# Two tiles of x on ScalarE's load queue, more softmax buffers and another order of the instructions in a fused attention and dense kernel

## The chip, the cores and the metric

The kernel runs on one core of a Trainium2 chip. The metric is device time in microseconds (us). A core has five engines that each work through a queue of their own in order: TensorE (matmuls; PE in the profile, its weight loads PEld), VectorE (DVE), ScalarE (ACT), GpSimd (POOL) and SyncE (SP, which here only issues DMAs). Sixteen DMA engines move the data. SP and ScalarE can both issue loads, each on a queue of its own.

## The reference

The input x has 2048 tokens of 512 features (bf16). After a layer norm without scale, two branches are added to x:

```python
xn = layernorm(x)
# A: linear attention, 32 heads of 16 features
q, k, v = split(xn @ wqkv)
phi(t)  = concat(softmax(t @ w_phi), softmax(-(t @ w_phi)))     # per head, 16 + 16
kv  = sum over tokens of phi(k)^T v;   z = sum over tokens of phi(k)
o   = (phi(q) @ kv) / (phi(q) . z + 1e-6)
A   = o @ wo
# B: dense layer with mish
h   = xn @ w1 + b1              # 1792 features
B   = (h * tanh(softplus(h))) @ w2
out = x + A + B
```

## The kernel before

The tokens stand in 16 tiles of 128. Four tiles form a group g. TensorE needs xn with features on the partitions (`xnT`); for group 0 it is turned by TensorE itself (TP, L557) and copied out of PSUM (TC, L564), for the other groups by DMA (`ln_turn_dma`, L185, part of AP).

The matrix w_phi is folded into the weights of q and k: `load_turned` (L140) loads 512 columns of wqkv transposed by a DMA into `wT`, F0 and F (L152) multiply it with `Wbd`, a block diagonal matrix that WB (L523) makes of w_phi, and FD and FC (L164) copy the products into `wkp` and `wqk`. Logits of tile i and softmax group s (0 to 3 keys, 4 to 7 queries) then are one product (L, L246; LP for the first two tiles at once, L202; WL for two tiles of group 1), copied by LC.

Each softmax group goes through E (maximum and minimum, and differences from them), X (exponentials, ScalarE), S (sums, L302, VectorE), R (inverses, L325) or W (weights for the queries, L347), N (products). A collects kv on TensorE; KV masks it. Of the queries, W ends with two DMA transposes (L290), Q multiplies with kv, G copies the results, C divides and turns them by DMA (L440). H is one block of 128 of the 1792 hidden features for one group (56 in all), M its mish on ScalarE. O is the second dense layer of a tile, P adds the attention's projection, Y adds x and stores. The last tile is done in two parts (OH, PH, YH). V and VC are the values, LN and AP statistics and normalisation of groups 1 to 3; for group 0, LS, RS and AZ do the same tile by tile. PB and CB turn the bias b1, DX loads groups 2 and 3 of x, DW 2 and DW 3 load w2 and wo, WT loads the q columns of wqkv transposed, KM makes a mask.

The order of all this is a list written out (`STEPS`, L24): every step emits its instructions to its engines at that place, so each engine's queue has the order of the list. A number behind @ is the PSUM bank (six in rotation, each of 512 columns); a or v says whether ScalarE or VectorE does a copy or an inverse. A step waits only for its data and for its bank or buffer to come free. Ahead of the list stand the first loads and twelve matmuls on constants (L511):

```python
    nc.sync.dma_start(x_sb[:, 0, :], x_v[:, 0, :])
    wT_of = {0: load_turned(D)}
    ...
        nc.scalar.dma_start(wsrc[:], wphi_v)
    nc.scalar.dma_start(x_sb[:, 1, :], x_v[:, 1, :])
    nc.scalar.dma_start(b1b[:], b1_v[:, :])
    nc.sync.dma_start(x_sb[:, 2:4, :], x_v[:, 2:4, :])
    nc.sync.dma_start(wv[:], wqkv_v[:, :, 2 * D : 3 * D])
    nc.sync.dma_start(w1_sb[:, :, 0 : 7 * P], w1_v[:, :, 0 : 7 * P])
    nc.sync.dma_start(x_sb[:, 4:8, :], x_v[:, 4:8, :])
    nc.sync.dma_start(w1_sb[:, :, 7 * P : F], w1_v[:, :, 7 * P : F])
```

The old list begins: LS 0; RS 0; DX 2; LS 1; WB; RS 1; AZ 0; TP 0; F0 0; F0 1; AZ 1; FD 0 v; TP 1; TC 1 v; LS 2; PB; RS 2; TC 0 a; LS 3; RS 3; FD 1 a; AZ 2; F0 2; F0 3; FD 2 a; FD 3 a; LP; KM; DX 3; AZ 3; V 0; LC 0 0 a; TP 2; V 1; TC 2 a; TP 3; VC 0 a; LC 0 1 v; TC 3 v; CB; L 0 2; L 0 3; LC 0 3 a; LN 1; H 0; H 1; H 2; M 0.

Of the kernel before, what the change touches and what calls it, by code (L numbers as in the profile page):

```python
# [8 lines left out]
BF16 = mybir.dt.bfloat16  # L9
# [12 lines left out]

WARM = 12
STEPS = """  # L24
LS 0; RS 0; DX 2; LS 1; WB; RS 1; AZ 0; TP 0 @0; F0 0 @1; F0 1 @2; AZ 1; FD 0 v; TP 1 @3; TC 1 v; LS
2; PB @4; RS 2; TC 0 a; LS 3; RS 3; FD 1 a; AZ 2; F0 2 @5; F0 3 @0; FD 2 a; FD 3 a; LP i @1,2; KM;
DX 3; AZ 3; V 0 @3; LC 0 0 a; TP 2 @5; V 1 @0; TC 2 a; TP 3 @1; VC 0 a; LC 0 1 v; TC 3 v; CB; L 0 2
@5; L 0 3 @2; LC 0 3 a; LN 1; H 0 @3; H 1 @1; H 2 @4; M 0; LC 0 2 a; H 3 @2; M 1; M 2; M 3; VC 1 a;
E 0 0; H 4 @3; H 5 @5; AP 1 0; H 6 @1; H 7 @4; M 4; H 8 @2; M 5; H 9 @0; M 6; M 7; H 10 @3; M 8; M
9; M 10; AP 1 1; H 11 @5; E 0 1; V 4 @1; X 0 1; WL 1; LN 2; V 6 @4; VC 4 a; X 0 0; L 1 0 @2; L 1 3  # L30
@0; LC 1 0 a; V 5 @3; LN 3; VC 5 a; H 12 @1; WL 2; H 13 @2; VC 6 a; S 0 0; LC 1 3 a; M 11; V 3 @3; M
12; M 13; H 14 @4; H 15 @0; H 16 @5; H 17 @1; VC 3 a; M 14; H 18 @2; M 15; M 16; M 17; LC 1 2 a; H
19 @3; AP 2 0; AP 2 1; AP 3 0; L 2 0 @4; LC 2 0 a; L 2 1 @0; LC 2 1 a; V 2 @5; S 0 1; L 2 2 @1; M
18; LC 1 1 a; M 19; H 20 @4; LC 2 2 a; AP 3 1; H 21 @0; WT; H 22 @2; M 20; VC 2 a; R 0 1 v; L 2 3
@3; H 23 @1; R 0 0 v; N 0 1; M 21; N 0 0; H 24 @4; M 22; LC 2 3 a; F 0 @5; F 1 @0; E 1 0; E 1 1; M
23; M 24; F 2 @2; E 2 0; E 2 1; FC 0 a; H 25 @3; H 26 @1; FC 1 a; H 27 @4; M 25; M 26; L 3 2 @5; FC
2 a; M 27; V 7 @0; L 3 3 @3; V 11 @1; F 3 @2; L 3 0 @4; LC 3 0 v; LC 3 2 a; L 3 1 @5; A 0 0; X 1 0;
X 1 1; A 0 1; LC 3 3 a; FC 3 v; S 1 0; V 8 @4; LC 3 1 a; VC 7 a; L 4 0 @2; E 3 0; VC 8 a; LC 4 0 a;
L 4 1 @3; LC 4 1 a; L 4 3 @5; VC 11 a; L 4 2 @0; X 2 0; V 9 @4; L 5 0 @2; H 28 @3; H 29 @1; VC 9 a;
LC 4 2 v; M 28; M 29; H 30 @0; H 31 @4; H 32 @3; M 30; H 33 @1; H 34 @0; M 31; M 32; M 33; M 34; H  # L40
35 @4; M 35; H 36 @3; M 36; S 1 1; LC 4 3 a; R 1 0 v; E 3 1; LC 5 0 a; N 1 0; R 1 1 v; H 37 @1; H 38
@0; H 39 @4; H 40 @3; H 41 @5; H 42 @2; S 2 0; A 1 0; M 37; N 1 1; M 38; M 39; M 40; A 1 1; M 41; M
42; X 3 0; L 6 3 @1; L 5 2 @0; V 10 @4; VC 10 a; L 5 1 @3; LC 5 2 a; L 6 0 @5; E 4 0; E 4 1; X 2 1;
S 3 0; V 15 @2; VC 15 a; V 13 @4; VC 13 a; LC 6 0 a; R 2 0 a; S 2 1; DW 3; R 3 0 a; X 3 1; L 6 1 @0;
LC 5 1 a; DW 2; N 3 0; N 2 0; L 5 3 @2; O 0 @4; S 3 1; V 12 @5; V 14 @3; LC 6 1 a; LC 5 3 a; O 1 @0;
L 6 2 @2; R 2 1 a; N 2 1; VC 14 a; LC 6 3 a; VC 12 v; R 3 1 a; N 3 1; X 4 0; A 2 0; S 4 0; LC 6 2 a;
A 2 1; A 3 0; W 4 0 v; X 4 1; H 43 @3; M 43; A 3 1; H 44 @1; H 45 @5; M 44; H 46 @2; M 45; H 47 @3;
M 46; M 47; H 48 @1; KV; H 49 @5; H 50 @2; Q 0 0; M 48; M 49; G 0 0; M 50; H 51 @3; H 52 @1; H 53
@5; S 4 1; W 4 1 v; M 51; M 52; H 54 @2; H 55 @3; Q 0 1; M 53; E 5 0; E 5 1; M 54; E 6 0; L 7 0 @1;
M 55; G 0 1; C 0 a; X 5 0; LC 7 0 a; L 7 1 @5; X 5 1; O 2 @2; O 3 @3; LC 7 1 a; L 7 2 @1; LC 7 2 a;  # L50
S 5 0; Q 1 0; L 7 3 @5; G 1 0; E 6 1; W 5 0 a; P 0; P 1; Y 0; Q 1 1; O 4 @1; G 1 1; LC 7 3 a; O 5
@4; S 5 1; Q 2 0; O 6 @5; C 1 a; P 2; G 2 0; W 5 1 v; Y 1; Q 2 1; P 3; O 7 @0; E 7 0; X 6 0; S 6 0;
G 2 1; Q 3 0; C 2 a; G 3 0; Y 2; Y 3; X 6 1; O 8 @2; Q 3 1; W 6 0 v; E 7 1; S 6 1; P 4; P 5; G 3 1;
C 3 a; Q 4 0; X 7 0; Y 4; W 6 1 v; X 7 1; S 7 0; O 9 @3; O 10 @1; G 4 0; Q 4 1; P 6; P 7; G 4 1; Y
5; Y 6; C 4 a; Q 5 0; W 7 0 a; G 5 0; O 11 @4; Q 5 1; Y 7; O 12 @5; S 7 1; G 5 1; C 5 a; Q 6 0; G 6
0; O 13 @0; Q 6 1; G 6 1; W 7 1 v; P 8; P 9; Q 7 0; C 6 a; G 7 0; P 10; P 11; Y 8; Q 7 1; G 7 1; O
14 @2; Y 9; Y 10; C 7 a; P 12; P 13; OH 0 @3; PH 0; Y 11; P 14; OH 1 @1; PH 1; Y 12; Y 13; YH 0; Y
14; YH 1
"""


# [1 line left out]
def kernel(  # L63
# [12 lines left out]
    nc = tc.nc  # L76
# [146 lines left out]
    def hidden(u, b):  # L223
# [3 lines left out]
        for kt in range(KT):  # L227
# [5 lines left out]
                stop=(kt == KT - 1),  # L233
            )

    def mish(u):
        g, f = divmod(u, FT)
        table("mish")
        nc.scalar.activation(  # L239
            acts[:, f, g * 512 : (g + 1) * 512], ph_of.pop(u)[:], ACT.Mish, bias=b1f[:, f : f + 1]  # L240
        )
# [59 lines left out]

    def sums(s, k):  # L302

        t = s_of[s, k] = smx.tile([P, 128], FP32, name="s", bufs=3)
        nc.vector.reduce_sum(  # L305
            t[:], pair(s, k).rearrange("p t j l (c e) -> p (t j l c) e", e=16), axis=AX.X
        )
# [7 lines left out]
            out, src.rearrange("p (c o) -> p c o", o=1).to_broadcast([P, n, 2]), ACT.Exp, scale=scale  # L315
        )

    def log(src, n):

        table("natural_log_exp_and_others")  # L320
        t = smx.tile([P, 128], FP32, name="log")
        nc.scalar.activation(t[:, 0:n], src, ACT.Ln)
        return t[:, 0:n]

    def invert(s, k, how):  # L325

        t = s_of.pop((s, k))
        r2 = r_of[s, k] = smx.tile([P, 128, 2], BF16, name="r2")
        if how == "a":
            power(r2[:], log(t[:], 128), 128, -1.0)  # L330
            return
        r = smx.tile([P, 128], BF16, name="r")
        with nc.allow_low_precision("the softmaxes are bf16"):
            nc.vector.reciprocal(r[:], t[:])
        nc.vector.tensor_copy(r2[:], r[:].rearrange("p (c o) -> p c o", o=1).to_broadcast([P, 128, 2]))
# [9 lines left out]
    def weigh(s, k, how):  # L345

        t = s_of.pop((s, k))  # L347
        q = smx.tile([P, 16, 4], FP32, name="q")
        r2 = smx.tile([P, 16, 4, 2], BF16, name="q2")
        if how == "a":  # L350
            t4 = log(t[:], 128).rearrange("p (t l c) -> p t l c", l=2, c=4)
            nc.vector.tensor_tensor(
                out=q[:], in0=t4[:, :, 0, :], in1=t4[:, :, 1, :], op=ALU.subtract
            )
            power(r2[:].rearrange("p t c o -> p (t c) o"), q[:].rearrange("p t c -> p (t c)"), 64, 1.0)
        else:
            t4 = t[:].rearrange("p (t l c) -> p t l c", l=2, c=4)
            nc.vector.reciprocal(q[:], t4[:, :, 1, :])
            nc.vector.tensor_tensor(
                out=r2[:], in0=t4[:, :, 0, :, None].to_broadcast([P, 16, 4, 2]),  # L360
                in1=q[:, :, :, None].to_broadcast([P, 16, 4, 2]), op=ALU.mult,
            )
        vv = pair(s, k).rearrange("p t j l c -> p (t j) l c")[:, :, 1, :].rearrange(
            "p t (c e o) -> p t c e o", e=8, o=2
        )
        nc.vector.tensor_tensor(
            out=vv, in0=vv, in1=r2[:, :, :, None, :].to_broadcast([P, 16, 4, 8, 2]), op=ALU.mult
        )
        turn(s, k)
# [70 lines left out]
    def combine(h, how):  # L440

        nm, ds = nd_of.pop(h)
        oT_of[h] = xnT[:, 2 * h : 2 * h + 2, :, :].rearrange("p t k c -> p (t k) c")
        f = opool.tile([P, 64, 2], BF16, name="f")
        d = ds[:].rearrange("p i j c -> p (i j c)")
        if how == "a":
            power(f[:], log(d, 64), 64, -1.0)
        else:
            w = opool.tile([P, 64], FP32, name="w")
            nc.vector.reciprocal(w[:], d)  # L450
            nc.vector.tensor_copy(
                f[:], w[:].rearrange("p (c o) -> p c o", o=1).to_broadcast([P, 64, 2])
            )
        v = nm.rearrange("p i j (c e o) -> p (i j c) e o", e=8, o=2)
        nc.vector.tensor_tensor(
            out=v, in0=v, in1=f[:, :, None, :].to_broadcast([P, 64, 8, 2]), op=ALU.mult
        )
        nc.sync.dma_start_transpose(out=oT_of[h], in_=nm.rearrange("p i j c -> p (i j c)"))
# [26 lines left out]
    with nc.allow_non_contiguous_dma(reason="tiny w_phi load"):  # L485
        nc.scalar.dma_start(wsrc[:], wphi_v)
    nc.scalar.dma_start(x_sb[:, 1, :], x_v[:, 1, :])
    nc.scalar.dma_start(b1b[:], b1_v[:, :])
    nc.sync.dma_start(x_sb[:, 2:4, :], x_v[:, 2:4, :])
    nc.sync.dma_start(wv[:], wqkv_v[:, :, 2 * D : 3 * D])  # L490
    nc.sync.dma_start(w1_sb[:, :, 0 : 7 * P], w1_v[:, :, 0 : 7 * P])
    nc.sync.dma_start(x_sb[:, 4:8, :], x_v[:, 4:8, :])
# [71 lines left out]
    def first_keep(i, copy):  # L564
        copy(xnT[:, i, :, :], pf_of.pop(("t", i))[:].rearrange("p (k c) -> p k c", k=KT))

    def stats(g):
        ln_of[g] = moments_of()
        st, mv, rstd = ln_of[g]
# [30 lines left out]
    def load_queries():  # L600
# [8 lines left out]
        "LN": stats, "AP": apply, "DX": load_tokens, "DW": load_weights, "WL": wide,  # L609
        "L": logits, "LC": lambda s, i, c: take(s, i, copies[c]),  # L610
        "V": value, "VC": lambda t, c: keep(t, copies[c]),
        "H": hidden, "M": mish,
        "E": extremes, "X": exponentials, "S": sums,
        "R": invert, "N": normalise, "A": accumulate,
        "KV": mask_kv, "W": weigh, "Q": attend, "G": gather, "C": combine,
# [40 lines left out]
```

## Time and profile before

| | |
|---|---|
| Runs | 173.78, 173.88, 173.98 us, median 173.88 |
| Profiled execution | 174.0 us |
| Its span (first to last instruction) | 172.3 us |
| TensorE clock granted (mean) | 1.00 |
| Busy: PE, DVE, ACT, POOL | 168.7, 143.2, 119.5, 9.4 us |
| Read from HBM, written | 6.84 MB, 2.10 MB |

The page gives busy times of the engines, the chain of work that ended last, the costliest groups of instructions and the DMA issues. The trace behind it answers for stretches of time, single lines, waits and loads. In lists of instructions the first column is the start in us from the beginning of the span, the second the length; in brackets stands the idle time before and what ended it. "DMA to landing" is from the issue to the moment that the data can be used.

### The profile page before, as it was taken

How to read it: one execution, taken by the hardware profiler on the slowest of the kernel's cores; microseconds unless marked ns; L12 is line 12 of the kernel's file. 1: busy time of each engine (PE TensorE's matmuls, PEld its weight loads, DVE VectorE, ACT ScalarE, POOL GpSimd, SP SyncE). 2: the span in 40 equal slices, each digit the busy share in tenths (PEclk: the TensorE clock that was granted, in tenths of full speed). 3: DMA queues.
4: the chain of work that ended last, by engine and by line, in shares of the span. 5: the costliest groups of instructions: out<-in, count | busy, mean ns of one | idle time of the engine just before them, and what ended most of it. 6: DMA issues, size and time to landing. Idle time of an engine off the chain costs nothing.

```text
span 172.3 us, 2713 instructions
## 1 busy us (share of the span) xinstructions
PE 168.7 (98%) x1039; PEld 82.4 (48%) x1039; DVE 143.2 (83%) x221; ACT 119.5 (69%) x192; POOL 9.4 (5%) x26
## 2 busy tenths in 40 slices
PE   8999999999999999999999999999999999999993
PEld 2554444444545444454446544444444545445452
DVE  2878998999997999979999999799988996844433
ACT  2446889979899998989999988974063883414200
POOL 4332205000000000000000000000000000000000
PEclk9999999999999999999999999999999999999999
DMA  5999350199930000000000363023974749885641
GB/s 98 269 377 365 82 98 0 37 189 207 366 120 0 0 4 0 0 0 0 4 0 0 64 118 66 12 51 67 150 152 93 150 95 144 172 168 100 173 134 61
DMA packets 44953, 18.02 MB, mean 105 GB/s; under 512 B 37004, under 2 KB 44940, under 8 KB 44940
## 3 DMA queue, kind: packets, MB, share of 16 engines
q1 hardware_dynamic: 44096, 17.60, 44.5%
q10 hardware_dynamic: 844, 0.25, 0.6%
q8 instruction: 8, 0.13, 0.3%
q14 instruction: 5, 0.04, 0.1%
HBM read 6.84 MB, written 2.10 MB: 52 GB/s over the span
## 4 chain that ended last, share of the span: by engine, by line
PE 95%; DMA 3%; SPq 0%; DVE 0%; issue 0%
PE po L463 28%; PE ph L228 28%; PE pl L194 14%; PE po L470 8%; PE pv L194 8%; DMA wT<-in_A_wqkv_dram 3%; PE pnd L418 2%; PE pkv L387 2%; PE pfold L156 1%; PE pwide L194 1%; PE pl L209 1%; PE ptr L560 0%; SPq L483 0%; DVE x_sb L477 0%; PE pb L533 0%
## 5 line engine op out<-in xcount | busy, mean ns | idle before, releaser
L463 PE MATMUL po<-w_sb,acts 128*128 128x512 bf16 (+2 forms) x238 | 50.7, 366 | 0.0
L228 PE MATMUL ph<-xnT,w_sb 128*128 128x512 bf16 x224 | 50.1, 379 | 0.0
L239 ACT ACTIVATE acts<-ph,b1f 128x512 bf16<-128x512 f32 x56 | 37.2, 694 | 4.6 <-PE ph L228 4.4
L305 DVE TENSOR_REDUCE s<-e 128x128 f32<-128x2048 bf16 x16 | 36.4, 2279 | 2.5 <-ACT e L288 2.5
L228 PEld LDWEIGHTS <-w_sb 128*128 128x128 bf16 x224 | 21.7, 98 | 25.5
L463 PEld LDWEIGHTS <-acts 128*128 128x128 bf16 x238 | 22.3, 98 | 24.1
L288 ACT ACTIVATE e<-e 128x2048 bf16<-128x2048 bf16 x16 | 30.3, 1908 | 0.0
L194 PEld LDWEIGHTS <-xnT 128*128 128x128 bf16 x184 | 17.6, 98 | 20.1 <-DMA wv<-in_A_wqkv_dram 0.2
L252 ACT CAST p_sb<-pl 128x512 bf16<-128x512 f32 x27 | 15.4, 587 | 5.5 <-PE pl L194 4.7
L433 ACT COPY ds<-pnd 128x32 f32<-128x32 f32 x16 | 2.9, 183 | 23.5 <-PE pnd L418 23.5
L194 PE MATMUL pv<-wv,xnT 128*128 128x512 bf16 x64 | 16.1, 379 | 0.0
L477 DVE TENSOR_TENSOR x_sb<-po,x_sb 128x512 bf16<-128x512 f32 (+2 forms) x17 | 10.9, 654 | 5.7 <-PE po L470 5.7
L470 PE MATMUL po<-wqk,xnT 128*128 128x512 bf16 (+2 forms) x68 | 15.5, 366 | 0.0
L194 PE MATMUL pl<-wqk,xnT 128*128 128x512 bf16 x64 | 15.3, 379 | 0.0
L170 DVE BATCH_NORM_STATS2 stats<-x_sb 128x6 f32<-128x512 bf16 x16 | 10.1, 679 | 4.3 <-DMA x_sb<-in_A_x_dram 4.3
L263 DVE TENSOR_TENSOR m<-m 128x512 bf16<-128x512 bf16 (+1 forms) x32 | 11.5, 358 | 1.1
L194 PE MATMUL pl<-wkp,xnT 128*128 128x512 bf16 x48 | 11.7, 379 | 0.0
L263 DVE TENSOR_TENSOR m<-p_sb 128x1024 bf16<-128x1024 bf16 x16 | 10.9, 682 | 0.2 <-ACT p_sb L252 0.2
L272 DVE TENSOR_TENSOR e<-p_sb,m 128x2048 bf16<-128x2048 bf16 x8 | 9.8, 1226 | 1.4 <-PE pkv L387 1.1
L272 DVE TENSOR_TENSOR e<-m,p_sb 128x2048 bf16<-128x2048 bf16 x8 | 9.8, 1225 | 0.3
L340 DVE TENSOR_TENSOR e<-e,r 128x2048 bf16<-128x2048 bf16 x8 | 9.6, 1215 | 0.0
L138 ACT ACT_TABLE_LOAD x7 | 9.0, 1283 | 0.1
(62 smaller groups left out, 131.4 us busy)
## 6 DMA issues: line engine op xcount, KB each, us to landing
out_dram<-x_sb SPq DMA_DIRECT2D x15, 128.0 KB, 2.0
w_sb<-in_B_w_dram SPq DMA_DIRECT2D x2, 896.0 KB, 7.8
x_sb<-in_A_x_dram SPq DMA_DIRECT2D x3, 512.0 KB, 10.0
w_sb<-in_B_w_dram SPq DMA_DIRECT2D x2, 640.0 KB, 8.8
wv<-in_A_wqkv_dram SPq DMA_DIRECT2D x1, 512.0 KB, 4.5
wqk<-in_A_wo_dram SPq DMA_DIRECT2D x1, 512.0 KB, 4.6
w_sb<-in_B_w_dram SPq DMA_DIRECT2D x1, 512.0 KB, 9.6
x_sb<-in_A_x_dram SPq DMA_DIRECT2D x1, 256.0 KB, 3.2
```

The costliest lines, as they stand in the source:

```text
L170: nc.vector.bn_stats(stats[:, i, :], xs[:, i, :])
L194: nc.tensor.matmul(pp, lhsT=xnT[:, t, kt, :], rhs=w[:, kt, :], start=(kt == 0), stop=(kt == KT - 1),)
L228: nc.tensor.matmul(ph_of[u][:], lhsT=w1_sb[:, kt, f * P : (f + 1) * P], rhs=xnT[:, g * TPG : (g + 1) * TPG, kt, :], start=(kt == 0), stop= ...
L239: nc.scalar.activation(acts[:, f, g * 512 : (g + 1) * 512], ph_of.pop(u)[:], ACT.Mish, bias=b1f[:, f : f + 1])
L252: copy(p_of[s][:, i, :], pl_of.pop((s, i)))
L263: nc.vector.tensor_tensor(out=m[:], in0=src[:, :, 0:half], in1=src[:, :, half : 2 * half], op=op)
L272: nc.vector.tensor_tensor(out=e_of[s][:].rearrange("p t j l c -> p (t j) l c")[:, :, pl, :].rearrange("p t (c e o) -> p t c e o", e=8, o=2 ...
L288: nc.scalar.activation(v, v, ACT.Exp)
L305: nc.vector.reduce_sum(t[:], pair(s, k).rearrange("p t j l (c e) -> p (t j l c) e", e=16), axis=AX.X)
L463: nc.tensor.matmul(po_of[t, c.stop][:, c], lhsT=acts[:, f, t * P : (t + 1) * P], rhs=w2_sb[:, f, c], start=(f == 0), stop=False,)
L470: nc.tensor.matmul(po_of[t, c.stop][:, c], lhsT=oT_of[t // 2][:, t % 2 * 4 + j, :], rhs=wo_sb[:, j, c], start=False, stop=(j == 3),)
L477: nc.vector.tensor_tensor(out=y, in0=po_of.pop((t, c.stop))[:, c], in1=y, op=ALU.add)
```

## The change

Tiles 2 and 3 of x are loaded from ScalarE's queue, behind tile 1, and the bias behind them; they had been on SP's queue between wT and wv. The sums `s` get six buffers instead of three, `r2` three instead of two, `r` one instead of two; `log` works in place instead of into a tile of its own. Two functions are new (`hidden_half`, `first_turn_dma`) and used by no step. The list has the same 433 steps in another order, with other banks and, for some, the other engine: R 1 0, R 1 1, W 6 0 and FC 3 go to ScalarE; C 0, W 5 0 and W 7 0 to VectorE; of the copies TC 2, VC 2, VC 4 and VC 5, FD 2, LC 3 1 and LC 4 3 are now VectorE's, and VC 12, FD 0, LC 0 1 and LC 3 0 are ScalarE's.

```diff
 STEPS = """
+DX 2; LS 0; WB; DX 3; LS 1; RS 0; RS 1; AZ 0; TP 0 @0; LS 2; AZ 1; TP 1 @1; F0 0 @2; F0 1 @3; F0 2
+@4; LS 3; RS 2; AZ 2; RS 3; TC 1 v; TC 0 a; FD 0 a; FD 2 v; F0 3 @5; AZ 3; TP 2 @0; FD 1 a; FD 3 a;
+TC 2 v; LP i @2,1; TP 3 @3; TC 3 v; V 0 @4; PB @5; H 0 @0; LC 0 0 a; CB; LC 0 1 a; V 3 @2; VC 3 a; M
+0; L 0 2 @3; LN 1; LC 0 2 a; L 0 3 @1; LC 0 3 a; V 1 @5; H 1 @2; H 2 @0; DW 3; H 3 @3; H 4 @1; M 1;
+M 2; M 3; M 4; VC 0 a; H 5 @2; LN 2; H 6 @0; M 5; AP 1 0; H 7 @3; H 8 @1; AP 1 1; M 6; M 7; VC 1 a;
+H 9 @4; H 10 @2; H 11 @0; M 8; E 0 0; M 9; M 10; M 11; E 0 1; AP 2 0; H 12 @3; H 13 @5; L 1 0 @1; V
...
+0; Q 6 1; P 8; W 7 1 v; Y 8; G 6 1; P 9; P 10; Q 7 0; C 6 a; P 11; G 7 0; Y 9; Q 7 1; O 14 @3; P 12;
+P 13; Y 10; Y 11; OH 0 @2; G 7 1; C 7 a; P 14; PH 0; OH 1 @0; PH 1; Y 12; Y 13; Y 14; YH 0; YH 1
 """
...
-        t = s_of[s, k] = smx.tile([P, 128], FP32, name="s", bufs=3)
+        t = s_of[s, k] = smx.tile([P, 128], FP32, name="s", bufs=6)
...
-    def log(src, n):
+    def log(v):
 
         table("natural_log_exp_and_others")
-        t = smx.tile([P, 128], FP32, name="log")
-        nc.scalar.activation(t[:, 0:n], src, ACT.Ln)
-        return t[:, 0:n]
+        nc.scalar.activation(v, v, ACT.Ln)
+        return v
...
-        r2 = r_of[s, k] = smx.tile([P, 128, 2], BF16, name="r2")
+        r2 = r_of[s, k] = smx.tile([P, 128, 2], BF16, name="r2", bufs=3)
         if how == "a":
-            power(r2[:], log(t[:], 128), 128, -1.0)
+            power(r2[:], log(t[:]), 128, -1.0)
             return
-        r = smx.tile([P, 128], BF16, name="r")
+        r = smx.tile([P, 128], BF16, name="r", bufs=1)
...
     nc.scalar.dma_start(x_sb[:, 1, :], x_v[:, 1, :])
+    nc.scalar.dma_start(x_sb[:, 2:4, :], x_v[:, 2:4, :])
     nc.scalar.dma_start(b1b[:], b1_v[:, :])
-    nc.sync.dma_start(x_sb[:, 2:4, :], x_v[:, 2:4, :])
     nc.sync.dma_start(wv[:], wqkv_v[:, :, 2 * D : 3 * D])
```

In the old list wo's load (DW 3) comes behind S 2 1 and the load of w2 (DW 2) behind LC 5 1; in the new one DW 3 stands behind H 2 and DW 2 behind M 15. The transposed load WT comes right behind AP 3 1 instead of one H later.

The end of the old list, for comparison: Q 6 1; G 6 1; W 7 1 v; P 8; P 9; Q 7 0; C 6 a; G 7 0; P 10; P 11; Y 8; Q 7 1; G 7 1; O 14; Y 9; Y 10; C 7 a; P 12; P 13; OH 0; PH 0; Y 11; P 14; OH 1; PH 1; Y 12; Y 13; YH 0; Y 14; YH 1.

More of the change, by code (lines that the diff above doesn't have):

```diff
@@ L24 @@
 STEPS = """
[L25 to L58, printed above, removed]
+DX 2; LS 0; WB; DX 3; LS 1; RS 0; RS 1; AZ 0; TP 0 @0; LS 2; AZ 1; TP 1 @1; F0 0 @2; F0 1 @3; F0 2
+@4; LS 3; RS 2; AZ 2; RS 3; TC 1 v; TC 0 a; FD 0 a; FD 2 v; F0 3 @5; AZ 3; TP 2 @0; FD 1 a; FD 3 a;
@@ new lines @@
+TC 2 v; LP i @2,1; TP 3 @3; TC 3 v; V 0 @4; PB @5; H 0 @0; LC 0 0 a; CB; LC 0 1 a; V 3 @2; VC 3 a; M
+0; L 0 2 @3; LN 1; LC 0 2 a; L 0 3 @1; LC 0 3 a; V 1 @5; H 1 @2; H 2 @0; DW 3; H 3 @3; H 4 @1; M 1;
+M 2; M 3; M 4; VC 0 a; H 5 @2; LN 2; H 6 @0; M 5; AP 1 0; H 7 @3; H 8 @1; AP 1 1; M 6; M 7; VC 1 a;
+H 9 @4; H 10 @2; H 11 @0; M 8; E 0 0; M 9; M 10; M 11; E 0 1; AP 2 0; H 12 @3; H 13 @5; L 1 0 @1; V
+4 @4; LN 3; VC 4 v; M 12; V 2 @2; VC 2 v; X 0 1; AP 2 1; AP 3 0; AP 3 1; WT; X 0 0; S 0 0; WL 1; WL
@@ new lines @@
+2; S 0 1; L 1 3 @0; M 13; H 14 @3; H 15 @4; H 16 @2; M 14; LC 1 0 a; L 2 1 @5; M 15; DW 2; H 17 @3;
+H 18 @1; M 16; M 17; M 18; LC 1 3 a; H 19 @4; L 2 0 @2; M 19; LC 1 1 a; H 20 @3; H 21 @1; M 20; H 22
+@0; H 23 @4; LC 2 0 a; M 21; M 22; LC 1 2 a; R 0 0 v; M 23; H 24 @3; H 25 @2; LC 2 1 a; R 0 1 v; F 0
+@1; H 26 @0; M 24; M 25; F 1 @4; M 26; FC 0 a; L 2 2 @5; LC 2 2 a; N 0 0; FC 1 a; L 2 3 @3; LC 2 3
+a; F 2 @2; H 27 @0; M 27; FC 2 a; H 28 @1; M 28; E 1 0; H 29 @5; F 3 @4; A 0 0; M 29; E 1 1; N 0 1;
@@ new lines @@
+FC 3 a; E 2 0; L 3 0 @3; X 1 0; V 7 @0; V 6 @2; E 2 1; A 0 1; VC 7 a; V 10 @1; V 11 @5; LC 3 0 a; VC
+6 a; V 5 @4; VC 5 v; S 1 0; VC 11 a; L 4 1 @0; VC 10 a; X 1 1; L 4 0 @3; H 30 @2; L 3 1 @5; LC 4 0
+a; LC 3 1 v; X 2 0; L 4 3 @1; LC 4 3 v; V 8 @4; L 3 3 @3; S 1 1; L 3 2 @5; VC 8 a; R 1 0 a; N 1 0;
+LC 3 2 a; R 1 1 a; L 4 2 @1; LC 4 2 v; LC 3 3 a; M 30; H 31 @4; H 32 @5; M 31; M 32; A 1 0; H 33 @3;
+H 34 @1; M 33; V 13 @2; LC 4 1 a; M 34; H 35 @4; M 35; H 36 @5; KM; E 3 0; H 37 @3; H 38 @0; H 39
@@ new lines @@
+@1; H 40 @4; M 36; M 37; M 38; VC 13 a; S 2 0; N 1 1; M 39; M 40; H 41 @5; H 42 @3; M 41; A 1 1; M
+42; V 9 @0; E 3 1; X 3 1; L 5 0 @2; E 4 0; LC 5 0 a; L 5 1 @1; X 2 1; LC 5 1 a; E 4 1; O 0 @4; O 1
+@5; S 3 1; VC 9 a; X 3 0; L 5 3 @3; X 4 0; L 6 0 @2; V 14 @1; LC 6 0 a; S 2 1; S 3 0; VC 14 a; L 6 3
+@0; LC 6 3 a; R 2 0 a; L 6 1 @2; LC 5 3 a; L 6 2 @1; S 4 0; N 2 0; R 2 1 a; W 4 0 v; V 12 @0; LC 6 1
+a; R 3 1 a; O 2 @3; LC 6 2 a; V 15 @2; N 2 1; R 3 0 a; N 3 0; VC 12 a; L 5 2 @1; N 3 1; X 4 1; S 4
@@ new lines @@
+1; H 43 @0; VC 15 a; A 2 0; A 2 1; A 3 0; M 43; H 44 @2; LC 5 2 a; A 3 1; H 45 @0; M 44; M 45; H 46
+@1; H 47 @2; H 48 @0; M 46; M 47; M 48; KV; H 49 @1; M 49; Q 0 0; G 0 0; W 4 1 v; H 50 @2; M 50; H
+51 @0; Q 0 1; G 0 1; H 52 @1; M 51; M 52; H 53 @2; M 53; H 54 @0; M 54; H 55 @1; M 55; Q 1 0; L 7 0
+@2; G 1 0; L 7 2 @0; L 7 1 @1; Q 1 1; E 5 0; E 5 1; LC 7 0 a; LC 7 2 a; O 3 @2; X 5 0; C 0 v; E 6 0;
+LC 7 1 a; E 6 1; G 1 1; O 4 @0; O 5 @1; P 0; S 5 0; C 1 a; X 6 0; P 1; P 2; P 3; W 5 0 v; Q 2 0; S 6
@@ new lines @@
+0; X 5 1; Y 0; X 6 1; Y 1; S 5 1; W 5 1 v; L 7 3 @4; G 2 0; LC 7 3 a; O 6 @5; Y 2; Q 2 1; E 7 0; G 2
+1; C 2 a; O 7 @4; Y 3; O 8 @3; Q 3 0; W 6 0 a; O 9 @2; E 7 1; S 6 1; G 3 0; Q 3 1; P 4; Y 4; G 3 1;
+P 5; Q 4 0; C 3 a; W 6 1 v; O 10 @0; Y 5; X 7 0; G 4 0; Q 4 1; G 4 1; S 7 0; C 4 a; W 7 0 v; X 7 1;
+O 11 @1; Q 5 0; P 6; Y 6; P 7; G 5 0; S 7 1; Q 5 1; Y 7; G 5 1; O 12 @5; C 5 a; Q 6 0; O 13 @4; G 6
+0; Q 6 1; P 8; W 7 1 v; Y 8; G 6 1; P 9; P 10; Q 7 0; C 6 a; P 11; G 7 0; Y 9; Q 7 1; O 14 @3; P 12;
@@ L234, in hidden, with hidden_half @@
             )
+    def hidden_half(u, i, b=None):
+        if i == 0:
+            ph_of[u] = bank(b, "ph")
+        for kt in range(KT):
+            nc.tensor.matmul(
+                ph_of[u][:, i * 256 : (i + 1) * 256],
+                lhsT=w1_sb[:, kt, u * P : (u + 1) * P],
+                rhs=xnT[:, 2 * i : 2 * i + 2, kt, :],
+                start=(kt == 0),
+                stop=(kt == KT - 1),
+            )
     def mish(u):
@@ L350, in weigh @@
         if how == "a":
-            t4 = log(t[:], 128).rearrange("p (t l c) -> p t l c", l=2, c=4)
+            t4 = log(t[:]).rearrange("p (t l c) -> p t l c", l=2, c=4)
             nc.vector.tensor_tensor(
@@ L446, in combine @@
         if how == "a":
-            power(f[:], log(d, 64), 64, -1.0)
+            power(f[:], log(d), 64, -1.0)
         else:
@@ L565, in first_keep, with first_turn_dma @@
         copy(xnT[:, i, :, :], pf_of.pop(("t", i))[:].rearrange("p (k c) -> p k c", k=KT))
+    def first_turn_dma(i):
+        nc.scalar.dma_start_transpose(out=xnT[:, i, :, :], in_=xn_of[0][:, i, :])
     def stats(g):
@@ L611 @@
         "V": value, "VC": lambda t, c: keep(t, copies[c]),
-        "H": hidden, "M": mish,
+        "H": hidden, "M": mish, "AD": first_turn_dma,
+        "HA": lambda u, b: hidden_half(u, 0, b), "HB": lambda u: hidden_half(u, 1),
         "E": extremes, "X": exponentials, "S": sums,
```

## The prediction

> A difference of about 0.2%, 0.35 us here, is what a measurement of this kernel can tell from no change.
>
> **What bounds the kernel now.** First the page: how busy TensorE is, and what the chain that ended last is made of.
>
> ```profile
> span 172.3 us, 2713 instructions
> PE 168.7 (98%) x1039; PEld 82.4 (48%) x1039; DVE 143.2 (83%) x221; ACT 119.5 (69%) x192; POOL 9.4 (5%) x26
> ...
> PE 95%; DMA 3%; SPq 0%; DVE 0%; issue 0%
> ```
>
> A busy TensorE alone proves little, because ends of matmuls are modelled; the chain does. It is one DMA and then TensorE to the end. The same chain in order of time, first 16 us (start, length, what):
>
> ```profile
> 1.25 5.36 DMA wT<-in_A_wqkv_dram
> 6.61 0.05 issue
> 6.65 0.62 PE pfold L156 x8
> ...
> 12.06 1.73 PE pl L194 x8
> 13.78 2.38 PE ph L228 x11
> ```
>
> From 6.65 to 169.65 us nothing but TensorE pieces follow one another, each kind always at the same length (four matmuls of 512 columns: 0.86 us). So TensorE has no idle time to give back in the middle. A new order can gain only ahead of 6.65 us or behind the last matmul, and it loses wherever TensorE waits for something new. All 433 steps occur in both orders, with the same matmuls; so I only have to find TensorE's waits, and these sit at the head, where its inputs still arrive. VectorE's timeline there (start, length, operation):
>
> ```profile
> 3.18 0.69 DVE L170 BATCH_NORM_STATS2 stats<-x_sb 128x6 f32<-128x512 bf16 x1 [3.18 <-DMA x_sb<-in_A_x_dram]
> 3.91 0.18 DVE L172 BATCH_NORM_AGGREGATE mv<-stats 128x2 f32<-128x6 f32 x1
> 4.41 0.69 DVE L170 BATCH_NORM_STATS2 stats<-x_sb 128x6 f32<-128x512 bf16 x1 [0.32 <-DMA x_sb<-in_A_x_dram]
> 5.14 0.18 DVE L172 BATCH_NORM_AGGREGATE mv<-stats 128x2 f32<-128x6 f32 x1
> 5.24 0.41 DVE L524 TENSOR_TENSOR Wbd<-block,wsrc 128x512 bf16<-128x512 bf16 x1
> 5.57 0.41 DVE L181 TENSOR_SCALAR xn<-x_sb,mv,rstd 128x512 bf16<-128x512 bf16 x1
> 6.45 0.41 DVE L181 TENSOR_SCALAR xn<-x_sb,mv,rstd 128x512 bf16<-128x512 bf16 x1 [0.48 <-POOL rstd L177]
> ```
>
> Starts follow each other by 0.83 for statistics with their aggregate (4.41 to 5.24) and by 0.33 for Wbd or one AZ. The second AZ waits for GpSimd's root, ready at 6.42. Last, the loads: issues with size and landing time after issue, and the share of the 16 DMA engines in half microseconds (the last two columns).
>
> ```profile
> x_sb<-in_A_x_dram SPq DMA_DIRECT2D x1, 128.0 KB, 2.4
> x_sb<-in_A_x_dram ACTq DMA_DIRECT2D x1, 128.0 KB, 3.1
> ```
> ```profile
> L491 SPq DMA_DIRECT2D w_sb<-in_B_w_dram x1: 507/507/507, 5.5 to 5.5; - x1
> ...
> DMA to landing us min/median/max: 6.4/6.4/6.4
> ```
> ```profile
> 3.00:3.50 0.50, 0.50 (x3) 0.21 (x2) 0.32 (x1) 0.50 (x1) 0.00 (x0) 1.00 0.72 183
> 3.50:4.00 0.50, 0.50 (x3) 0.15 (x1) 0.47 (x2) 0.32 (x1) 0.00 (x0) 1.00 1.02 90
> 6.00:6.50 0.50, 0.50 (x5) 0.34 (x4) 0.05 (x1) 0.00 (x0) 0.42 (x1) 1.00 0.55 161
> 7.00:7.50 0.50, 0.50 (x10) 0.40 (x7) 0.41 (x1) 0.38 (x2) 0.00 (x0) 1.00 0.73 211
> ```
>
> The first half of w1 lands at 5.54 + 6.4 = 11.94. In the old order its first user, H 0, starts its first matmul at 13.62, so 1.7 us of cover.
>
> **The head in the new order.** TensorE does TP 0, TP 1, F0 0 to 3, TP 2, LP, TP 3, V 0, PB, H 0. Compared with the old order, L 0 2, L 0 3 and V 1 now come behind H 0: three groups of 0.864. With the same pace H 0 would start at 13.62 - 2.59 = 11.03. Every later start is a loss that TensorE, full to the end, cannot make good.
>
> First I ask when TensorE arrives. VectorE: LS 0 3.18, WB 4.01, LS 1 4.41 (tile 1 lands then, as before), AZ 0 5.24, LS 2 5.57 if tiles 2 and 3 have landed, AZ 1 6.45 (LS 2 needs until 6.40, the root until 6.42), ready at 6.86. So TP 1 runs 6.91 to 7.13, no earlier than before, but the folds now queue behind it: from 7.13 instead of 6.65. Sixteen matmuls at 0.056 end at 8.03. LS 3 (6.78) and AZ 2 (7.61 to 8.02) let TP 2 run 8.07 to 8.29; TC 1 ends at 8.36, FD 2 at 8.96 on VectorE; FD 0, 1, 3 (0.58 each, from 7.56) end at 8.15, 8.73 and 9.31 on ScalarE. LP needs the third one at 8.78 at the earliest and then runs through to 10.08; TP 3 to 10.30, V 0 to 11.17, PB a little: TensorE arrives at H 0 at 11.25. Against 11.03 that is +0.22. The fold's delay of 0.48 shrinks because TP 1 and TP 2 are already done and PB waits.
>
> Then the inputs. Tiles 2 and 3 (256 KB) are issued on ScalarE's queue at 1.83, where b1b was, 2.6 us before their place on SP (4.42). Their landing is not in the trace. Lower bound: 1.83 + 3.1 = 4.9, by tile 1's row; upper bound: with wT at its latest, 6.6 + 0.75 = 7.4. The 0.75 is 256 KB at the 350 GB/s that the loads reach between 8 and 9 us. I take 5.6, nearest the tile 1 row plus the second 0.75: LS 2 then starts without a wait worth counting. Each 0.1 later is 0.1 more.
>
> wT shares the engines with this load. Bounds: 6.61 as now, 7.36 with the whole 0.75 added. The rows of 3 to 4 us show a share of 0.72 and 1.02, so some is free, not all: I take 7.0, which TP 1 at 6.91 to 7.13 hides. The Trainium skill, "DMA: Bandwidth & Descriptors", section "Queues, rings and completion order", says that each DMA engine takes packets in turn from the rows that have work, and under "Issuing engines are not separate DMA queues" that starting from two engines saves only issue time; by that rule alone wT pays all of the 0.75. The two tile rows of equal size, 2.4 against 3.1 us, lean the same way, and a case below is priced for it.
>
> w1: SP issues it 0.62 earlier (5.54 to 4.92), but the engines must move the same bytes ahead of it. Bounds: 11.94 as before (all slots were used), and 11.2 if all of the 0.75 fits into idle slots. Idle, from the shares of 3.0 to 3.5, 6.0 to 6.5 and 7.0 to 7.5: 0.14 + 0.22 + 0.13 = 0.5. I take a bit over half of that, 0.3: w1 lands at 11.65, H 0 starts at 11.70 (a fold starts 0.04 behind its DMA). This wait is new: 11.70 against an arrival of 11.25. Behind H 0 on TensorE are V 3, L 0 2 and all else. Sum of the head: 11.70 - 11.03 = +0.67.
>
> **The rest.** I walked every queue through the new order with the durations of the rows; the same walk on the old order gives VectorE's waits of the trace (4.45 against 4.35 before C 6's product). Edits at nothing: s, r2 and log buffers (no wait in the list of waits is for one, and the logarithms in place write as many elements as before); R 1 0 and R 1 1 on ScalarE (1.2 us off VectorE each, 0.73 on ScalarE, whose seven table loads stay seven); the other changed engines (C 0, W 5 0 to W 7 0, copies) trade at most 1.5 us between two engines that TensorE doesn't wait for. VectorE now does LN 2 ahead of E 0 0 and waits for its tiles (landing 7.4 + 10.0 = 17.4), so E 0 0 starts at 21.5 instead of 16.1; A 0 0 on TensorE at 50 still has over 2 us. wo's load (512 KB, 4.6 us) and its 0.5 of issue move on SP ahead of the xnT transposes; these are issued near 21, land near 24, and L 1 0 wants them at 27. The w2 loads move behind WT, and O 0 comes at 79. Bias: PB moved from 7.43 to 11.2, well behind its load. The tightest places: H 54 (0.0 to 0.1 spare), O 10 and O 12 (0.2), Q 7 1, which has one P of 0.86 instead of two between it and Q 7 0, while the two copies of G 7 0 are done 1.0 after a Q's start and Q with P takes 1.12. All at nothing; without their cover 0.1 to 0.3 each. The end, from the last matmul at 169.65 to 172.3, keeps YH 1; Y 14 ahead of YH 0 finishes both before it.
>
> **The sum.** The profiled execution took 174.0 us: 174.0 + 0.67 = 174.67. The runs' median is 173.88, 0.12 below that execution, so 174.55.
>
> **The rivals.** (1) The load is absorbed: the tiles land by 5.6, w1 at 11.2, and H 0 starts when TensorE arrives. For it: idle slots of 0.5 and the earlier issue. Against: shares at or over 1 from 3.5 to 6. Time: +0.22, 174.1, not slower by the bound; it decides if w1 lands before 11.35. 0.20. (2) The transposed load pays in full: wT 7.36, tiles 2 and 3 about 6.4, so AZ 1 and TP 1 come 0.8 later, arrival near 12.0, w1 at 11.94. Time: +1.0, 174.9. Chance 0.15. The rule of the Trainium skill named above, taken alone, is this case. (3) The head as forecast, and the tight places fail too, VectorE having lost its slack to LN 2's wait: 0.67 + up to 0.5, 175.0. 0.07. (4) The edit does nothing that TensorE sees, or gains by something outside the walk: with the folds behind TP 1 no path through the rows gets H 0 below 11.03, so a gain has only what the walk misses; one worth counting would give 173.4 or less. 0.08.
>
> **The numbers.** The forecast keeps 0.50: with (2) and (3) slower has 0.72, same 0.20 by (1), faster 0.08. The range goes from just under (1) to past (2) and (3): 173.9 to 175.2.
>
> **What would show it.** First group of pfold near 7.1 to 7.4, behind ptr; a wait of TensorE for w_sb ahead of the first ph matmul at 11.6 to 11.8; the chain naming w_sb's load instead of wT's; no other gap; the last matmul 0.7 later. Wrong if ph starts before 11.3 (w1 came early), if LS 2 starts after 6.2 (tiles late), or if gaps appear beyond 60 us.

## The result and the profile after

The changed kernel takes 178.21 us (median of 4 runs, 177.74 to 178.75) against 173.84 before. The ratio is 1.025, with a 95% interval of 1.021 to 1.029: slower by 4.4 us, far outside the range of the prediction. The profiled execution is the fastest of the four (177.74, span 176.0).

The span grew by 3.7 us. On the page, the chain that ended last no longer begins with wT, but with the load of x:

```profile
span 176.0 us, 2709 instructions
...
PE 169.7 (96%) x1039; PEld 83.6 (48%) x1039; DVE 143.6 (82%) x222; ACT 119.0 (68%) x190; POOL 9.3 (5%) x26
...
PEclk9969999999999999999999999999999999999999
...
PE 93%; DMA 3%; DVE 1%; ACTq 1%; issue 0%
```

Two things are to be seen: DVE and ScalarE's queue now stand in the chain, and PEclk has a 6 in its third slice where the page of before had nines throughout. The chain in order of time, from the load of tiles 2 and 3 to H 0 (start, length, what):

```profile
1.83 5.75 DMA x_sb<-in_A_x_dram
7.58 0.02 issue
7.61 0.70 DVE stats L169
8.31 0.02 issue
8.34 0.18 DVE mv L171
8.52 0.31 DVE xn L180
8.83 0.05 issue
8.88 0.61 PE ptr L571 x4
9.48 1.71 PE pfold L155 x16
11.19 0.43 PE ptr L571 x4
11.62 1.95 PE pl L208 x8
...
14.76 0.97 PE ph L227 x4
```

Tiles 2 and 3 land 5.75 us after their issue, at 7.58, no earlier than when SP issued them 2.6 us later (4.42 + 3.2 = 7.6). LS 2, the statistics at 7.61, waits for them, and behind it in VectorE's queue stands AZ 1 (8.44 to 8.82), which TP 1 (8.88) needs. TensorE had finished TP 0 by 6.07 and waits 2.81 us:

```profile
8.88 0.61 PE L571 MATMUL ptr<-ident,xn 128*128 128x128 bf16 x4 [2.81 <-DVE xn L180]
```

VectorE's idle time between AZ 0 and AZ 1 stands on one line:

```profile
5.20 0.41 DVE L180 TENSOR_SCALAR xn<-x_sb,mv,rstd 128x512 bf16<-128x512 bf16 x1
7.61 0.69 DVE L169 BATCH_NORM_STATS2 stats<-x_sb 128x6 f32<-128x512 bf16 x1 [2.00 <-DMA x_sb<-in_A_x_dram]
8.34 0.18 DVE L171 BATCH_NORM_AGGREGATE mv<-stats 128x2 f32<-128x6 f32 x1
8.44 0.38 DVE L180 TENSOR_SCALAR xn<-x_sb,mv,rstd 128x512 bf16<-128x512 bf16 x1
```

The second surprise is in the length of the pieces: sixteen matmuls of the fold take 1.71 us, 0.107 each, where before they took 0.056. The busy times by stretch say why (after the engines come the granted clock, the DMA share and GB/s):

```profile
5.00:8.50 3.50, 1.06 (x7) 0.36 (x5) 1.43 (x6) 0.59 (x1) 1.12 (x3) 1.00 1.22 214
8.50:12.00 3.50, 3.12 (x26) 2.84 (x27) 2.99 (x9) 1.66 (x3) 1.78 (x4) 0.51 1.07 369
12.00:14.00 2.00, 2.00 (x14) 1.00 (x12) 0.32 (x2) 0.61 (x2) 0.00 (x0) 1.00 1.09 359
```

From 5.0 to 8.5 TensorE was busy for 1.06 of 3.5 us at full clock; the next 3.4 us ran at half clock. The Trainium skill, "TensorE: Matmul & The Clock Gate", Part 1, says that the clock halves after an idle window of about 3.4 us. The trace agrees with that length in how long the half clock lasted, 3.4 us; but the wait was only 2.8 us, and the 3.5 us ahead of the half clock held 1.06 us of matmuls.

wT landed at 1.25 + 7.5 = 8.75 (6.61 before), w1 at 4.7 + 7.6 = 12.3 (11.94). Neither ended a wait here, because TP 1 at 8.88 and H 0 at 14.70 came later still; wT was only 0.5 us ahead of the first fold (9.28), so an earlier TP 1 would soon have met a wait for wT. (14.70 is H 0's start in the list of instructions; the chain above counts it from the modelled end of the piece ahead.) H 0's first matmul starts 3.67 us behind the 11.03 of an unchanged pace, and that is the whole loss. From there to the last matmul's end at 173.39 pass 158.7 us, as before: 169.65 - 13.62 + 2.59 = 158.6.

### The profile page after: what moved, and what is told of

Read it like the earlier page. It is cut to its first block, busy times and chain, and to the rows that moved or that the text cites. A ratio compares the mean times of both kernels' runs of the same rounds, so it can differ in the third digit from the quotient of the medians.

```text
span 176.0 us, 2709 instructions
## 1 busy us (share of the span) xinstructions
PE 169.7 (96%) x1039; PEld 83.6 (48%) x1039; DVE 143.6 (82%) x222; ACT 119.0 (68%) x190; POOL 9.3 (5%) x26
## 4 chain that ended last, share of the span: by engine, by line
PE 93%; DMA 3%; DVE 1%; ACTq 1%; issue 0%
PE ph L227 28%; PE po L474 27%; PE pl L193 14%; PE po L481 8%; PE pv L193 8%; DMA x_sb<-in_A_x_dram 3%; PE pnd L429 2%; PE pkv L398 2%; PE pfold L155 1%; PE pl L208 1%; PE pwide L193 1%; PE ptr L571 1%; DVE stats L169 0%; ACTq L498 0%; ACTq L497 0%; DVE xn L180 0%
## 5 line engine op out<-in xcount | busy, mean ns | idle before, releaser
L227 PE MATMUL ph<-xnT,w_sb 128*128 128x512 bf16 x224 | 51.0, 379 | 0.0
L251 ACT ACTIVATE acts<-ph,b1f 128x512 bf16<-128x512 f32 x56 | 37.7, 693 | 7.4 <-PE ph L227 7.3
L275 DVE TENSOR_TENSOR m<-m 128x512 bf16<-128x512 bf16 (+1 forms) x32 | 11.5, 359 | 1.1
L217 ACT CAST vext<-pv 128x512 bf16<-128x512 f32 x13 | 7.4, 587 | 3.1 <-PE pv L193 3.1
```

What stands on the lines that cost most here:

```text
L227: nc.tensor.matmul(ph_of[u][:], lhsT=w1_sb[:, kt, f * P : (f + 1) * P], rhs=xnT[:, g * TPG : (g + 1) * TPG, kt, :], start=(kt == 0), stop= ...
L251: nc.scalar.activation(acts[:, f, g * 512 : (g + 1) * 512], ph_of.pop(u)[:], ACT.Mish, bias=b1f[:, f : f + 1])
L275: nc.vector.tensor_tensor(out=m[:], in0=src[:, :, 0:half], in1=src[:, :, half : 2 * half], op=op)
```

## The experiments

Four readings were possible: the new order (LS 2 ahead of AZ 1) loses by itself; the load beside wT loses by itself; the half clock is a third loss; the rest of the new order has a loss or a gain of its own. Ratios are to the kernel before, measured beside each.

**The loads put back, the order kept.**

```diff
-    nc.scalar.dma_start(x_sb[:, 2:4, :], x_v[:, 2:4, :])
     nc.scalar.dma_start(b1b[:], b1_v[:, :])
+    nc.sync.dma_start(x_sb[:, 2:4, :], x_v[:, 2:4, :])
```

> The changed kernel with its new order, but tiles 2 and 3 of x loaded from SP's queue behind wT again. Theory 1 (the order: LS 2 stands ahead of AZ 1, and the tiles land near 7.6 on either queue, so AZ 1, TP 1 and all folds wait, and TensorE goes to half clock): LS 2 starts at 7.6, TP 1 near 8.9, H 0 near 14.7, time 177.2 to 178.2, as the changed kernel. Theory 2 (the queue: the load beside wT slows both, and the order would be harmless): wT lands at 6.6 again and the time falls to 175.5 or less.

177.44 us, ratio 1.020 (1.019 to 1.022). wT landed at 6.15, earlier than TensorE could use it, and the tiles at 7.3. VectorE waited for them as in the changed kernel:

```profile
7.30 0.69 DVE L169 BATCH_NORM_STATS2 stats<-x_sb 128x6 f32<-128x512 bf16 x1 [1.92 <-DMA x_sb<-in_A_x_dram]
```

TP 1 ran at 8.57, the clock halved, H 0 started at 14.29. So the order alone loses 3.5 us. Theory 2 alone falls.

**The new loads in the old order.** The same edit the other way round in the kernel before.

> The kernel before with its old order, but tiles 2 and 3 on ScalarE's queue behind tile 1 and the bias behind them. Theory 1 (only the order costs): 173.9, since nothing in the old order needs these tiles before 8. Theory 2 (the load beside wT slows both): wT lands near 8.4 instead of 6.6, the first fold starts 1.8 later and all behind it: 175.6, and up to 177 if TensorE's wait of 2.2 us also halves its clock.

179.41 us, ratio 1.031 (1.025 to 1.036). wT landed 9.3 us after its issue, at 10.55, and the first fold waited for it:

```profile
10.55 1.04 PE L156 MATMUL pfold<-Wbd,wT 128*128 128x128 bf16 x8 [2.60 <-DMA wT<-in_A_wqkv_dram]
```

Tile 1 came late too (1.28 + 4.4 = 5.7 instead of 4.4), and TensorE was at half clock from 6.9 to 13.7. So the queue alone loses 5.5 us, with runs from 177.85 to 180.37. "Only the order costs" falls as well, and theory 2 was too low: wT came over 2 us later than its 8.4, and the time is above its 177. That is more than both parts together cost in the changed kernel. One reason is that the waits lie over the same stretch: the new order is busy with its own wait while wT is late. The other is that wT landed at 8.75 in the changed kernel and at 10.55 here; why it differs with the same first loads no run shows.

**One swap in the changed kernel:** `AZ 0; TP 0; AZ 1; TP 1; LS 2` for `AZ 0; TP 0; LS 2; AZ 1; TP 1`.

> The changed kernel with one swap: AZ 1 and TP 1 ahead of LS 2 instead of behind. Theory 1: TP 1 runs at 6.9 again; if wT then landed at 6.6 to 7.0 the folds would follow and H 0 start near 12, 175.0. Theory 2: TP 1 at 6.9, but the folds wait for wT until 8.4, and TP 2 for LS 2 (7.6): H 0 near 13, 176 if the clock stays full, 177 if it halves.

179.97 us, ratio 1.034 (1.031 to 1.038). TP 1 ran at 6.73, as both theories had it; then TensorE waited for wT until 10.11, and half clock followed. Both theories missed: H 0 started at 16.20, not near 12 or 13. All four runs (179.26 to 180.47) are slower than the slowest of the changed kernel (178.75). In the profiled one wT took 8.8 us to land instead of 7.5, and the tiles came at 9.54 instead of 7.58; why they came later here is not shown. The swap takes TP 1's wait away and uncovers wT's.

**Both undone:** loads on SP and that swap.

> The changed kernel with both suspects undone: tiles 2 and 3 from SP's queue behind wT, and AZ 1 with TP 1 ahead of LS 2. If these two and the half clock make the whole loss but TP 2 still stands ahead of LP: wT lands near 6.3, TP 1 at 6.9, folds behind it, then TP 2 waits for LS 2 (tiles at 7.4), root and AZ 2 until 9.4, H 0 near 12.6: 175.5, and 176.5 if the clock halves. If something else in the new head costs: over 177.

176.19 us, ratio 1.015 (1.010 to 1.019). The folds run at full clock from 7.12; then TP 2 holds TensorE up:

```profile
7.12 1.06 PE L155 MATMUL pfold<-Wbd,wT 128*128 128x128 bf16 x16
9.94 0.40 PE L571 MATMUL ptr<-ident,xn 128*128 128x128 bf16 x4 [1.77 <-DVE xn L180]
10.18 1.89 PE L208 MATMUL pl<-wkp,xnT 128*128 128x512 bf16 x8
```

H 0 started at 13.20, 0.6 later than expected. By the medians the swap gives back 1.3 of the 3.5 us that the order loses with these loads. The other 2.2 remain because the new order asks for tile 2 (TP 2) ahead of LP, and LS 2 could not start before 7.57.

**Tiles 2 and 3 on SP ahead of wT,** with the new order:

```diff
     nc.sync.dma_start(x_sb[:, 0, :], x_v[:, 0, :])
+    nc.sync.dma_start(x_sb[:, 2:4, :], x_v[:, 2:4, :])
     wT_of = {0: load_turned(D)}
...
-    nc.scalar.dma_start(x_sb[:, 2:4, :], x_v[:, 2:4, :])
```

> The changed kernel, with tiles 2 and 3 loaded on SP ahead of wT, so that nothing large runs beside the transposed load. If running beside wT is what slowed both: the tiles land near 4.0 to 4.5, wT near 7.0, LS 2 and AZ 1 do not wait, H 0 starts near 11.7, 174.5, as the prediction had it for the change. If wT is slowed by the amount of data and not by running side by side: wT near 8.5, H 0 near 13, 176.

174.81 us, ratio 1.004 (1.003 to 1.006). The tiles landed at 4.65, wT at 6.7, w1 at 11.5; LS 2 had no wait, H 0 started at 11.90, and the clock stayed full. The other reading, that wT is slowed by the amount of data alone, falls: the same bytes ahead of wT left it at 5.0 us from issue to landing. With early tiles and an early wT the time comes close to the prediction (0.8 us above the kernel before, 0.67 forecast), but in part by luck: tile 1 landed at 5.0 instead of 4.4 and moved TP 1 to 7.47, 0.56 behind the forecast, while the wait for w1 that was to cost 0.45 did not come. From TP 1 to H 0 the walk held: 4.43 us against 4.34.

**The half clock by itself:** 13 more matmuls on constants behind TP 0 of the changed kernel, and 12 in the one with the loads put back. They fill TensorE's wait and do no part of the result.

> The changed kernel with 13 more matmuls on constants between TP 0 and TP 1, so that TensorE works through its wait of 2.8 us. They do no part of the result. If the half clock from 8.5 to 11.9 us costs time of its own: first fold 0.056 instead of 0.107 a matmul, LP earlier by 1.0 to 1.5, time 176.3 to 176.7, and its runs no longer differ by 0.9. If only the wait for the tiles counts: 177.7 as the changed kernel.

> The changed kernel with its loads on SP as before (tiles at 7.3 to 7.6) and 12 more matmuls on constants between TP 0 and TP 1, which do no part of the result; beside the run with the loads put back alone (177.4) it takes away only the half clock. If the half clock is worth its own time: folds at 0.056 a matmul, 176.0 to 176.5. If not: 177.4.

With the loads put back: 176.53 us, ratio 1.016 (1.014 to 1.018), against 177.44 without: 0.9 us less, though the tiles came 0.2 later (LS 2 at 7.53). The folds took 0.056 a matmul. In the changed kernel, where wT and the tiles vary, the runs took 176.78, 176.90, 178.12 and 179.67 us, ratio 1.019 (1.015 to 1.023, without the last), so that pair says little by its times, and the expectation that its runs would no longer differ was wrong. In its trace the clock is full, the tiles came 0.43 later, and H 0 starts at 13.74 instead of 14.70. The stretch from TP 1 to H 0, which holds no wait of TensorE in these traces, shows the half clock by itself: 5.82 us in the changed kernel and 5.72 with the loads put back, but 4.43 in both traces with the filling matmuls and in the one with the tiles ahead of wT. So the half clock costs 1.3 to 1.4 us of its own in the head.

**The old head, then the new rest.** The old loads and steps up to H 0, then the new list.

> The old loads and the old order up to H 0, then the rest of the new order (banks as the new list has them, the new buffers). If the whole loss sits in the head: 173.7 to 174.1, H 0 at 13.6. If the rest of the new order costs or gains: by as much above or below 173.9.

> As the kernel with the old head and the rest of the new order, with H 1 in bank 4 instead of bank 2, so that it needn't wait for VC 3 (the wait of 0.83 us at 16.05 there). If the rest of the new order is neutral: 173.6 to 174.1, within the measurement of before. If the rest itself costs: 174.3 or more.

The first gave 174.61, ratio 1.003 (1.002 to 1.005), with H 0 at 13.48 and one gap of 0.83 us at 16.05, made by the seam: H 1 had to wait for VC 3's bank. With H 1 in bank 4 it gave 173.94, ratio 1.0006 (0.9997 to 1.0016). The rest of the order, the buffers and the changed engines are worth nothing that can be measured.

**What slows wT.** Plain loads instead of the transposing one, first with all that SP issues behind it, then with that held back until VectorE is behind LS 1:

> The changed kernel with wT loaded plainly, 512 KB of the same columns, not transposed (so the folded key weights are not those of the reference; the amount of work is the same). If the transposing transfer is what a load beside it suffers from: tiles 2 and 3 land near 5, wT near 5.5, H 0 near 11.7, 174.5. If any 512 KB beside it does the same: tiles at 7 or later, 177.

> The changed kernel with wT loaded plainly (not transposed, so the folded key weights are not those of the reference), and with the loads behind it on SP (wv, w1, tiles 4 to 7) held until VectorE is behind LS 1, so that only wT and tiles 1 to 3 move together. If the transposition is what the side by side suffers from: tiles 2 and 3 land at 5.2 or earlier, wT at 5 or earlier. If any two loads on two queues do it: tiles at 6.5 or later. The time itself says little, since w1 comes later.

In the first (177.90, one run) the tiles landed at 7.9, but wv and w1 moved at the same time, so the tiles decide nothing; wT itself took only 4.5 us to land with all these loads beside it. In the second (177.24, one run) wT landed at 5.95 and the tiles at 6.63. By the written bounds the tiles speak for "any two loads on two queues"; wT itself, 2.8 us earlier than beside the same load when transposed, speaks for the transposition. The bandwidth tells more. The kernel before first, where no large load stands on ScalarE's queue after 4.4 us; then the changed kernel; then the held plain load; last two columns DMA share and GB/s:

```profile
4.00:5.00 1.00, 1.00 (x3) 0.29 (x2) 0.68 (x2) 0.00 (x0) 0.73 (x2) 1.00 1.17 183
5.00:6.00 1.00, 1.00 (x3) 0.15 (x1) 0.94 (x4) 0.00 (x0) 0.58 (x3) 1.00 1.41 274
```
```profile
4.00:5.00 1.00, 1.00 (x3) 0.30 (x2) 1.00 (x3) 0.35 (x1) 0.75 (x2) 1.00 1.13 197
5.00:6.00 1.00, 1.00 (x7) 0.36 (x5) 0.57 (x3) 0.00 (x0) 0.76 (x3) 1.00 1.27 181
```
```profile
4.00:5.00 1.00, 1.00 (x4) 0.35 (x3) 0.42 (x2) 0.34 (x1) 0.73 (x2) 1.00 1.09 384
5.00:6.00 1.00, 0.40 (x2) 0.00 (x0) 0.01 (x1) 0.00 (x0) 0.17 (x1) 1.00 0.99 342
```

In all three the engines count as fully busy, but the mixture with transposed packets moves half as much as two plain loads. Part of that is the transposing load's own: without a large load beside it, too, it moves 183 and 274 GB/s. With the load beside it the total is 197 and 181 in the changed kernel, and fell to 62 and 115 in the old order with the new loads. And it is shared: SP's queue, on which wT moves, got through 705 and 983 packets in these two microseconds before, and 344 and 412 in the changed kernel. The plain runs show a second effect: beside a plain wT the tiles took 4.8 us to land, against 3.2 to 3.7 on SP's queue, so a load on ScalarE's queue came in late beside a large one there without any transposition (one run). What in the engines causes either stays open.

**How much beside it.** The kernel before with tiles 4 to 7 (512 KB) on ScalarE's queue, and with only w_phi and the bias there (tiles 0 and 1 in one load on SP):

> The kernel before in its old order, but tiles 4 to 7 of x (512 KB) instead of tiles 2 and 3 moved to ScalarE's queue behind tile 1. If a load on the other queue slows wT by its amount: 256 KB made wT land 2.4 to 4 us later, so 512 KB make it land near 12, time 179 to 182. If the two queues only share turns until wT is done: wT near 9 as with 256 KB, 176 to 178.

> The kernel before in its old order, with tiles 0 and 1 of x in one load on SP ahead of wT, so that ScalarE's queue holds only w_phi and the bias while wT moves. If any load beside wT slows it: wT lands at 6.0 to 6.3 instead of 6.6, the first fold comes up to 0.4 earlier, 173.5 to 173.8. If 128 KB beside it cost nothing: wT at 6.6 or a little later, 173.9 to 174.2.

| On ScalarE's queue beside wT | wT, issue to landing |
|---|---|
| w_phi and bias | 4.5, 5.0 |
| with tile 1 (128 KB) | 5.4 before; 4.9 to 5.3 in six others |
| with tile 1 and 256 KB | 7.5, 7.8, 8.8, 9.3 |
| with tile 1 and 512 KB | 9.2 (179.36 us) |

The cost is not in proportion to the amount: 256 KB cost 2 to 4 us, 512 KB no more (one run), as if the load took turns for as long as wT lasts. The expectations had this case both ways: wT at 10.45 lies between their 9 and 12, close to the 10.55 that 256 KB gave in this order, and the time of 179.36 in the range of the one with wT near 12. For the 128 KB of tile 1 the rows show no clear price. The Trainium skill, "DMA: Bandwidth & Descriptors", "Queues, rings and completion order", has turns by packets. The traces agree with turns, since from 4 to 6 us of the changed kernel both queues moved packets (0.09 and 0.11 MB of SP's, 0.11 and 0.08 of ScalarE's), but not with the price equal to the load's own time that the prediction drew from them.

With tiles 0 and 1 in one load on SP wT landed at 5.8, earlier than expected, and yet the kernel took 174.15, ratio 1.0016 (1.0008 to 1.0025): the first fold started only 0.2 earlier (6.44), tile 0 came 0.6 later with tile 1 in its load, TP 0 ran at 6.21 and TP 1 at 7.10 (7.11 before), and H 0 started at 13.62 as before. So the next run has them as two loads, to see whether tile 1's way to TP 1 is the next limit:

> The kernel before in its old order, with tiles 0 and 1 of x as two loads on SP ahead of wT; ScalarE's queue holds only w_phi and the bias. Tile 0 lands at 3.2 as before, tile 1 near 3.8 instead of 4.4, wT near 6.2. If tile 1's way to TP 1 is what is late next: AZ 1 near 6.1 instead of 6.45, LP near 7.7 instead of 8.0, 173.4 to 173.6. If wT or the copies out of PSUM still set LP: 173.8 to 174.0.

174.08 us, ratio 1.0009 (0.9999 to 1.002): tile 1 landed at 4.3, not 3.8, and wT at 6.7, so neither came earlier and the reading stays untested. No version beat the kernel before.

## Why the prediction was wrong

- **Bound and method: right.** TensorE has no slack from the first fold on, and the head's delay appears one to one at the end: H 0 late by 3.67, span longer by 3.7.
- **The rest at nothing: right.** 158.7 against 158.6 us by the traces, ratio 1.0006 by the run with the old head. None of the tight places opened: from H 0 to the last matmul the chain of the changed kernel is TensorE without a gap.
- **The tiles' landing: the step that failed.** I took 5.6, from tile 1's 3.1 us plus the load's own 0.75; the upper end was 7.4. It was 7.58 in the profile and up to 9.7 in other kernels with these loads. The row of tile 1 was no neighbour: in the kernel before ScalarE's queue moved 0.12 MB from 2 to 3 us and 0.03 from 3 to 4, so tile 1 was largely through before wT's packets came, as this load was not. LS 2 at 7.61 instead of 5.57 moved TP 1 from 6.91 to 8.88: 1.97 us. The prediction named a start of LS 2 after 6.2 as a sign of being wrong, and had 7.4 as its own upper bound. By its slope (each 0.1 later is 0.1 more) 7.4 gives H 0 at 13.1 and a time near 175.9, past the end of its range at 175.2: the range left out a case that its working allowed.
- **wT's delay: mis-sized.** The term was 0 to 0.75 and I took 0.4; it was 2.1 to 3.9. I had reasoned with moved bytes at full rate, while the rows of 3 to 4 us in the profile of before (share 1.02 at 90 GB/s) already showed engines that were busy without moving much. Nor is a share of 1 the limit against which idle slots can be counted, since the same profile has 1.41 from 5 to 6 us. In this order wT's delay is covered by TP 1's; in the old order it is, with the late tile 1 and the half clock that follows, the loss.
- **The clock: missing.** The prediction looked at TensorE's waits only as lost time. The wait of 2.8 us halved its clock: from TP 1 to H 0 5.82 us (8.88 to 14.70) instead of the 4.34 that I walked (6.91 to 11.25). At full clock the runs took 4.43, so 1.39 is the clock's and 0.09 the walk's.
- **The w1 wait: did not decide.** It was 0.45 of the forecast 0.67. w1 landed at 12.3, long before H 0's turn. Where the tiles came early, H 0 started at 11.90 behind TensorE's own work (w1 at 11.5).
- Sum from the arrival at 11.25: 1.97 for the tiles, 1.39 for the clock and 0.09 for the walk give 14.70, the measured start of H 0. Rival (2) had the direction, late tiles and a late wT, and gave it a chance of 0.15 and 1.0 us, because its sizes came from the same two terms, tile 1's row and the load's own 0.75 us, and it had no half clock.

## What to carry to other kernels

Before a load is moved to a second queue, ask what it will run beside; here a load that shared its time with a large transposing one landed no earlier than when it was queued behind it 2.6 us later, and it delayed the large one by 2.1 to 3.9 us, where its bytes at full rate are 0.75. In an in-order queue, put work on data that lands late behind the work that the critical engine needs next: here LS 2 ahead of AZ 1 and TP 2 ahead of LP together cost 3.5 us. And a wait of TensorE can cost more than itself: here 2.8 us of wait brought 1.3 to 1.4 more at half clock.

## What the hardware showed that I had not expected

- DMA engines with a share of 1.13 to 1.27 moved 169 to 197 GB/s between 4 and 7 us with a transposing and a plain load side by side, against 342 to 384 for two plain loads, and 183 and 274 from 4 to 6 us for the transposing load without a large one beside it.
- A wait of 2.8 us halved TensorE's clock from 8.5 to 11.9 us, with 1.06 us of matmuls in the 3.5 us ahead. With the plain wT held alone, waits of 1.9 and 0.8 us with 0.4 us of matmuls between them halved it too; in the run with both parts undone, waits of 0.8 and 1.8 us with 1.3 us of matmuls between them left it full. Each stretch at half clock lasted 3.41 to 3.42 us in six traces, and 6.83 in the one of the new loads in the old order.
